# A delta-rule recurrence followed by a gated FFN: the first g @ w_out for four units at once, and the inverses of units 8 and 9 spread over three slots

## The chip, the core and the metric

The kernel runs on one core of a Trainium2 chip. The metric is the device time of one execution in microseconds, from the first to the last instruction and the little that lies around them. The engines are named as in the profile: PE is TensorE's matmul side and PEld its weight loads, DVE is VectorE, ACT is ScalarE, POOL is GpSimd, SP is the engine whose queue issues most DMAs. Each engine works through its own queue in order and waits on semaphores.

## The reference, cut to what matters

Four batches, eight heads, 768 time steps, head dimension 48, then an FFN over 3072 tokens with width 384 and hidden width 2048. The weights come in double precision.

```python
k_n = k / (np.linalg.norm(k, axis=-1, keepdims=True) + 1e-06)
for t in range(S):
    y[:, :, t] = einsum('bhd,bhde->bhe', q[:, :, t], state)
    v_old = einsum('bhde,bhd->bhe', state, k_n[:, :, t])
    state = state + beta_t * einsum('bhd,bhe->bhde', k_n[:, :, t], v[:, :, t] - v_old)
x = y.transpose(0, 2, 1, 3).reshape(B * S, H * D)
h = x @ w_in
g = h * (1.0 / (1.0 + np.exp(-1.702 * h)))
return g @ w_out
```

## The kernel before

**Units.** The recurrence is cut into chunks of 128 steps. A unit is one chunk of one batch, so there are 24 units, in the order chunk first, batch second: units 0 to 3 are chunk 0 of the four batches, 4 to 7 chunk 1, 8 to 11 chunk 2. Inside a unit, a Gram matrix G of the keys is made on PE (`prepare`, `gram`), its four 32 by 32 diagonal blocks per head go through DRAM into a tile NT with one block per partition, DVE inverts them there (`invert`: mostly pairs of a multiply into P and a sum out of P, 25 steps for chunk 2, for two batches at a time), and the inverses come back through DRAM as XB. "Blocks sent" in this document means G's way to NT (`Nd<-G` and `NT<-Nd`).

**A step.** `Step` does one unit: `scores` gives psQ (queries times keys, and keys times state), from which V and the masked matrix M come; then four rounds of `solve` (psU, from XB and V, copied to US by ACT) and `below` (psR, from G and U, subtracted from V by DVE); then `queries` and `outputs` make psY, from which the rows of x (xT) and the new state ST come.

**Slots.** `woven(n)` is one slot of the steady loop. It mixes the last rounds of unit n-1 (A), the middle rounds of unit n (B_) and the scores and first round of unit n+1 (D_), prepares unit n+5 (P, K), takes some steps of an inverse (`ahead_of`, numbers in `STEPS`), and fills the rest of PE's time with FFN work taken from `queue` by `spend`. Slots 3 to 6 take FFN work of cost 13.0 each, later slots 20.8. The order on each engine is the order in which the code records it: the wrapped engines `vec`, `act`, `pe`, `pool` and the wrapped DMA calls `sync` (SP's queue), `beside` (ACT's queue) and `other_queue` (POOL's queue) are pinned to program order.

**The FFN.** `hidden` makes ph = x @ w_in for 256 tokens (two units) and ACT's sigmoid-GELU writes it to gT tiles. `written` makes po = g @ w_out for one unit after another, 16 matmuls each. The queue begins with the rest of `hidden` for units 0 to 3, then `both_written` for units 0 and 1, then `written` for units 2 and 3.

**The weights.** They are turned from double to single precision on the core, piece by piece: `conversions` is a generator of DVE and ACT instructions for w_in's pieces and then for the 16 blocks of w_out, one block being 128 hidden rows by 384. `fill(n)` takes n steps of it; a block is about five steps. `both_written` goes through the blocks feature by feature: for each block it lets the conversion run until the block three ahead is done, and then issues one po matmul for each of two units. `fetch_out` brings a raw block in by DMA; later blocks need the place of earlier ones, and are fetched when those are converted (the table `fetches`), the first eight through POOL's queue and the others through SP's.

**PSUM.** There are eight banks: two in `ps_big` (psT, the first psQ pair, psG), four in `ps_seq` (psU, psR, the second psQ pair, psY), two in `ps_moe` (ph, po).

Of the kernel before, what the change touches and what calls it, by code (L numbers as in the profile page):

```python
# [18 lines left out]
def kernel(  # L19
# [47 lines left out]
    io = ctx.enter_context(tc.tile_pool(name="io", bufs=3))  # L67
    wk = ctx.enter_context(tc.tile_pool(name="wk", bufs=2))
    ps_big = ctx.enter_context(tc.tile_pool(name="ps_big", bufs=2, space=PSUM))
    ps_seq = ctx.enter_context(tc.tile_pool(name="ps_seq", bufs=4, space=PSUM))  # L70
    ps_moe = ctx.enter_context(tc.tile_pool(name="ps_moe", bufs=2, space=PSUM))
    dram = ctx.enter_context(tc.tile_pool(name="dram", bufs=2, space=bass.MemoryType.DRAM))

# [26 lines left out]
    def pinned(op):  # L100

        return lambda *a, **kw: tc.keep_in_program_order(op(*a, **kw))  # L102

    class Engine:

# [75 lines left out]
                )  # L181

    places, slots = {}, {}
    inside = {3: 6, 4: 8, 5: 10, 6: 12, 7: 14, 12: 14, 13: 10}
    outside = {0: "xT", 8: "xT", 11: "xT", 1: "M", 9: "M", 14: "M", 2: "M2", 10: "M2", 15: "M2"}
    order = [0, 1, 2, 3, 4, 5, 6, 7, 8, 13, 9, 10, 12, 11, 14, 15]

    def fetch_out(f):

        if f in outside:  # L190
            slot = outside[f]
            if slot not in slots:
                slots[slot] = wk.tile([128, 2 * DM], I32, tag=slot[:2].strip("2"), name="raw", bufs=3)
            words = slots[slot]
        else:
            words = raws[:, inside[f] * DM : (inside[f] + 2) * DM]
        places[f] = as_raw(words, (1, DM))
        first = order.index(f) < FC // 2
        (other_queue if first else sync)(
            out=as_rows(places[f])[:, 0], in_=moe_w_out[f * 128 : (f + 1) * 128, :]  # L200
        )

# [50 lines left out]
    def conversions():  # L253

        whole = list(pieces())

        def begin(i):
            dst, raw, shape, name = whole[i]
            ops = conversion(dst, places[name[1]] if raw is None else raw, shape)
            next(ops)  # L260
            return ops

        after = begin(0)
        yield
        for i in range(len(whole)):
            ops = after
            next(ops)
            yield
            next(ops)
            yield  # L270
            if i + 1 < len(whole):
                after = begin(i + 1)
                yield
            next(ops)
            yield
            next(ops)
            done.add(whole[i][3])
            fetches.pop(whole[i][3], lambda: None)()
            yield
# [1 line left out]
    fetches = {  # L281
        ("in", 0, 1): lambda: fetch_in(3),
        ("in", 3, 1): lambda: fetch_out(3),
        ("out", 4): lambda: fetch_out(13),
        ("out", 6): lambda: fetch_out(12),
    }
    for new, old in ((8, 0), (9, 1), (10, 2), (11, 8), (14, 9), (15, 10)):
        fetches[("out", old)] = lambda f=new: fetch_out(f)
    converting = conversions()

# [266 lines left out]


    def bank(name, shape=(128, H, D)):
        return ps_seq.tile(list(shape), F32, tag="seq", name=name)  # L560

    lasts = [None]

    class Step:
# [19 lines left out]
        def scores(self):  # L584

            c, S = self.c, slice(128, 128 + D)
            self.QS = (
                spare("QS")[:, 0 : NP * (128 + D)].rearrange("p (j t) -> p j t", j=NP) if self.n == B - 1
                else wk.tile([128, NP, 128 + D], F32, tag="QS", name="QS", bufs=3)
            )  # L590
            transposed(self.qp, self.QS[:, :, 0:128])
            if c > 0:
                St = ST[:, self.b, 0 : NP * D].rearrange("p (j d) -> p j d", j=NP)
                act.activation(self.QS[:, :, S], St, ACT.Copy)
            yield
            self.M = (
                spare("M").rearrange("p (h t) -> p h t", h=H) if self.n in (B - 1, B + 1)
                else wk.tile([128, H, 128], F32, tag="M", name="M", bufs=3)
            )
            n = 128 + D if c > 0 else 128  # L600
            for g in range(0, NP, 2):
                pool_, tag = (ps_seq, "seq") if g else (ps_big, "big")
                ps = [pool_.tile([128, 2, 128 + D], F32, tag=tag, name="psQ") for _ in range(2)]
                for i in range(2):
                    for hh in range(2):
                        r = self.rows(hh)
                        pe.matmul(
                            ps[hh][:, i, 0:n], lhsT=self.kT[r, g + i, :],
                            rhs=self.QS[r, g + i, 0:n], start=True, stop=True,
                        )  # L610
                for hh in range(2):
                    hs = slice(2 * g + hh, 2 * g + 4, 2)
                    if c > 0:
                        Vh = self.V[:, hs, :]
                        vec.tensor_tensor(Vh, Vh, ps[hh][:, :, S], op=ALU.subtract)
                    copy = act.copy if hh == 0 or self.n < 2 * B + HB else vec.tensor_copy
                    copy(self.M[:, hs, :], ps[hh][:, :, 0:128])
                if g == 0:
                    yield
            if self.n >= B:  # L620
                self.select()
# [146 lines left out]
            nc.sync.dma_start(out=out[b * S + c * C : b * S + (c + 1) * C, :], in_=o)  # L768
            yield 1.3

    def both_written(c, gT):

        po = [ps_moe.tile([128, DM], F32, tag="moe", name="po") for _ in range(HB)]
        for n, f in enumerate(order):
            ahead = order[min(n + 3, FC - 1)]
            while ("out", ahead - ahead % 2 if 4 <= ahead < 8 else ahead) not in done:
                fill(1)
            for i in range(HB):
                pe.matmul(
                    po[i], lhsT=gT[f // FQ][:, f % FQ, i * C : (i + 1) * C], rhs=w_out[:, f, :],  # L780
                    start=(n == 0), stop=(n == FC - 1),
                )
            if n < FC - 1:
                yield 1.3
        for i in range(HB):
            o = wk.tile([128, DM], F32, tag="o", name="o")
            act.copy(o, po[i])
            sync(out=out[i * S + c * C : i * S + (c + 1) * C, :], in_=o)
        yield 1.3

    def take(cost):
# [9 lines left out]
    def run(work):  # L801
        for _ in work:
            pass
# [61 lines left out]
            debt[0] -= done  # L865

    STEPS = (9, 5, 3, 3, 3, 3)
    begun = {}

    def woven(n, share):  # L870

        nonlocal inverting
        A, B_, D_ = steps.pop(n - 1, None), steps.get(n), steps.get(n + 1) or NoStep()
        m = n + B + 1
        if n < B + HB:
            K = normalize_mixed(m + 1) if n <= B else iter(())
        else:  # L880
            K = (normalize if n > 6 else normalize_mixed)(m) if m < len(units) else iter(())
        P = prepare(m) if m < len(units) else iter(())
        if m in begun:
            P = begun.pop(m)
        if n % HB == 1 and B < n and n + 1 + HB < len(units):
            inverting = invert(*units[n + 1 + HB], HB)
        ahead = STEPS[:3] if n % HB == 1 else STEPS[3:]

        next(K, None)
        together([(B_, 1)], [(A, 2)])  # L890
        run(D_.scored)
        next(K, None)
        ahead_of(inverting, ahead[0])
        spend(share / 3)

        together([(A, 3), (D_, 0)], [(B_, 1)])
        next(K, None)
        ahead_of(inverting, ahead[1])
        spend(share / 6)
        next(P, None)  # L900
        spend(share / 6)

        together([(B_, 2)], [(D_, 0)])
        if A:
            A.queries()
            A.outputs()
        run(P)
        ahead_of(inverting, ahead[2])
        if n % HB == 0:
            run(inverting)  # L910
        spend(share / 6)
        next(new_step(n + 2).scored, None)
        spend(share / 6)
        follow(n)
# [38 lines left out]
    late_U = room[:, 0 : H * D + XR]  # L953
    pool.memset(late_U[:, H * D :], 0.0)
    zs = room[:, 512 : 512 + 6 * B * H].rearrange("p (s b h) -> p s b h", s=6, b=B)
    psD = [ps_seq.tile([128, B, NP, BS], F32, tag="seq", name="psD") for _ in range(2)]
    warm(NW)
    for b in range(B):
        squares_first(b)
# [133 lines left out]
    load(B + 2, ((QP, q),), sync)  # L1093
    for n in range(2 * B + 1, 2 * B + 1 + HB):
        load(n, ((KN, k),), sync)
    for i in range(22):
        ahead_of(inverting, 1)
        if i < 18:
            feed()
        if i in (2, 3, 4, 7, 8, 9, 10):  # L1100
            fetch_out(i - 2 if i < 5 else i - 3)
    run(inverting)
    def beside_conversion(work):
        for cost in work:
            fill(2)
            yield cost

    queue = [beside_conversion(w) for w in ffn] + [both_written(0, gTs[0]), written(*units[HB], gTs[1])]
    for n in range(B - 1, len(units) + 1):
        woven(n, 20.8 if n > 6 else 13.0)  # L1110
    run(take(1e9))
# [31 lines left out]
```

## Time and profile before

| | us |
|---|---|
| median of 6 runs (772.1 to 779.09) | 773.0 |
| the profiled execution | 772.62 |
| its span, first to last instruction | 770.9 |
| PE busy / DVE busy / ACT busy / POOL busy in the span | 746.5 / 438.8 / 240.0 / 127.8 |
| mean granted PE clock | 0.970 of full |

The page splits the span into 40 slices and gives the busy tenths of each engine; a stretch of any length can be asked for by itself ("windows"). The timeline lists single instructions with start, duration and, in brackets, the idle time before them and what ended it. In the records a po, ph, psQ or psG matmul counts twice and a transpose (psT) once: a po group "x4" is two matmuls of the code.

By the timeline's first small solve of each slot, slot 3 begins at 126.38 us, slot 4 at 138.18, slot 5 at 161.53, slot 6 at 192.04 and slot 7 at 214.03. Before slot 3 lie the loading, the units 0 to 3 and most of the first `hidden`.

### The profile page before, as it was taken

The numbers are of one execution on the slowest core, as the hardware profiler recorded it, in microseconds if no ns is written. First come the engines' busy times: TensorE is split into PE (matmuls) and PEld (weight loads), VectorE is DVE, ScalarE is ACT, GpSimd is POOL, SyncE is SP. The second block draws the span as 40 slices with busy tenths as digits, with TensorE's granted clock in tenths as the row PEclk, the third lists the DMA queues.
The fourth block names the chain that finished last, engine by engine and source line by source line (L and its number), as shares of the span: only waits on it lengthen the run. The fifth ranks groups of instructions, "written<-read, shape, count | busy, mean of one in ns | idle before, by whom it ended". The sixth has DMA issues, their size and how long they took to land.

```text
span 770.9 us, 19471 instructions
## 1 busy us (share of the span) xinstructions
PE 746.5 (97%) x8508; PEld 559.9 (73%) x8508; DVE 438.8 (57%) x896; ACT 240.0 (31%) x535; POOL 127.8 (17%) x133
## 2 busy tenths in 40 slices
PE   7898999979999999999999999999999999999997
PEld 6677888546687687687678678678678677686774
DVE  6998897996776566566566566565566521000000
ACT  3566523433233133133133124123133132121110
POOL 6133301100222122121131221221210000000000
PEclk8599999999999999999999999999999999999999
DMA  9965355542142142142142142042030020000000
GB/s 167 171 120 111 93 135 124 141 107 78 44 97 57 37 94 56 36 96 56 34 96 57 33 98 56 22 108 57 22 78 11 23 43 2 17 11 1 26 1 21
DMA packets 131638, 50.79 MB, mean 66 GB/s; under 512 B 106432, under 2 KB 127040, under 8 KB 131552
## 3 DMA queue, kind: packets, MB, share of 16 engines
q1 hardware_dynamic: 129152, 41.27, 24.5%
q0 software_dynamic: 2400, 8.26, 4.2%
q8 instruction: 67, 1.10, 0.6%
q14 instruction: 19, 0.16, 0.1%
HBM read 32.08 MB, written 16.25 MB: 63 GB/s over the span
## 4 chain that ended last, share of the span: by engine, by line
PE 88%; DVE 7%; ACT 2%; issue 1%; POOL 0%; DVEq 0%; POOLq 0%; ACTq 0%
PE ph L102 32%; PE po L102 30%; PE psY L102 6%; PE psU L102 5%; PE psQ L102 5%; PE psG L102 4%; PE psR L102 3%; PE psT L102 3%; DVE w_out L102 2%; PE ps_warm L102 2%; DVE tmp L102 2%; DVE P L102 1%; DVE V L102 1%; DVE YB L102 1%; ACT QS L102 0%
## 5 line engine op out<-in xcount | busy, mean ns | idle before, releaser
L102 PE MATMUL po<-w_out,gT 128*128 128x384 f32 x768 | 265.5, 497 | 3.7 <-DVE w_out L102 3.7
L102 PE MATMUL ph<-xT,w_in 128*128 128x256 f32 x1152 | 261.2, 383 | 0.3
L102 PEld LDWEIGHTS ph<-xT,w_in 128*128 128x128 f32 x1152 | 214.8, 190 | 32.5 <-issue 1.7
L102 PEld LDWEIGHTS po<-w_out,gT 128*128 128x128 f32 x768 | 143.0, 192 | 97.4 <-issue 5.4
L102 DVE TENSOR_TENSOR V<-V,psR 128x384 f32<-128x384 f32 (+2 forms) x72 | 40.1, 557 | 194.3 <-PE psR L102 193.9
L102 ACT ACTIVATE gT<-ph 128x512 f32<-128x512 f32 x96 | 56.5, 596 | 150.7 <-PE ph L102 150.6
L102 ACT COPY US<-psU 32x384 f32<-32x384 f32 x92 | 43.2, 470 | 141.8 <-PE psR L102 76.9
L102 DVE TENSOR_TENSOR P<-NT,YB 64x8 f32<-64x8 f32 (+26 forms) x178 | 84.4, 474 | 4.7
L102 PEld LDWEIGHTS psU<-V,XB 32*32 32x32 f32 x1536 | 59.3, 106 | 35.6 <-issue 26.5
L102 DVE TENSOR_REDUCE YB<-P 64x4 f32<-64x8 f32 (+27 forms) x178 | 77.2, 434 | 6.2
L102 PE MATMUL psU<-V,XB 32*32 32x48 f32 x1536 | 70.4, 205 | 3.3 <-DVE V L102 3.3
L102 PE MATMUL psR<-US,G 32*32 32x48 f32 x2576 | 63.2, 205 | 0.5 <-ACT US L102 0.5
L624 POOL TENSOR_SCALAR_AFFINE_SELECT M<-M 128x1024 f32<-128x1024 f32 x20 | 25.5, 1273 | 222.8 <-DVE M L102 160.9
L102 PEld LDWEIGHTS psR<-US,G 32*32 32x32 f32 x2576 | 53.9, 105 | 1.3 <-ACT US L102 0.6
L102 PE MATMUL psQ<-QS,kT 48*128 48x176 f32 (+1 forms) x384 | 38.2, 344 | 5.4 <-ACT QS L102 5.4
L102 PEld LDWEIGHTS psQ<-QS,kT 48*128 48x128 f32 x384 | 31.2, 210 | 9.0 <-ACT QS L102 7.2
L102 DVE TENSOR_TENSOR P<-NT 64x256 f32<-64x256 f32 (+7 forms) x44 | 36.3, 824 | 0.3
L102 DVE TENSOR_REDUCE NT<-P 64x64 f32<-64x1024 f32 (+7 forms) x44 | 35.3, 803 | 1.5
L102 PE MATMUL psG<-kT 48*128 48x128 f32 x384 | 33.0, 311 | 1.4 <-ACT G L102 1.2
L102 ACT COPY o<-po 128x384 f32<-128x384 f32 x24 | 11.5, 479 | 72.5 <-issue 41.0
L87 POOL DMA_DIRECT2D KN<-in_k_dram x13 | 12.4, 953 | 118.0 <-PE psY L102 108.8
L102 ACT COPY M<-psQ 128x256 f32<-128x256 f32 x68 | 22.9, 377 | 26.5 <-DVE V L102 17.5
(102 smaller groups left out, 611.1 us busy)
## 6 DMA issues: line engine op xcount, KB each, us to landing
Nd<-G SPq DMA_DIRECT2D x16, 512.0 KB, 3.5
QP<-in_q_dram SPq DMA_DIRECT2D x24, 192.0 KB, 3.8
V<-in_v_dram SPq DMA_DIRECT2D x24, 192.0 KB, 3.1
out_dram<-o SPq DMA_DIRECT2D x24, 192.0 KB, 1.9
KN<-in_k_dram POOLq DMA_DIRECT2D x14, 192.0 KB, 3.7
NT<-Nd SPq DMA_DIRECT2D x20, 128.0 KB, 2.4
Yd<-YS SPq DMA_DIRECT2D x20, 128.0 KB, 2.4
XB<-Yd SPq DMA_DIRECT2D x20, 128.0 KB, 3.0
```

What stands on the lines that cost most here:

```text
L87: dma(out=dst[n % len(dst)][:, :, 0:D], in_=src[b, :, c * C : (c + 1) * C, :].rearrange("h p d -> p h d"),)
L102: return lambda *a, **kw: tc.keep_in_program_order(op(*a, **kw))
L624: (pool if self.n < B else nc.gpsimd).affine_select(out=self.M, in_=self.M, compare_op=ALU.is_gt, fill=0.0, base=0, pattern=[[0, H], [1, 1 ...
```

## The change

1. `both_written` becomes `all_written`: it holds four po tiles, and after each block of w_out it issues four po matmuls (units 0 to 3) where there were two. `written` for units 2 and 3 goes from the queue. The conversion is kept two blocks ahead, and `fill(3)` is taken after each pair of matmuls.
2. The two more po tiles take two of the four `ps_seq` banks. `ps_seq` becomes two pools of two banks. While `all_written` runs (`turns`), the steps have only the first pool for psU, psR, the second psQ pair and psY; otherwise they take the two pools in turn, one bank from each.
3. The four outputs are copied by ACT and sent through ACT's queue. All fetches of w_out go through POOL's queue; the order of the last eight blocks and the places that they use change, and two of them land in gT tiles that the first features leave free.
4. Unit 9's key norm (`ninth`) is made before slot 3 and its transpose, Gram matrix and blocks' way to NT in slot 3; unit 8's Gram matrix is made just ahead of slot 3. The inverse for units 8 and 9 begins in slot 4: `SOON` gives (0, 4, 5) steps in slot 4, (2, 3, 3) in slot 5 and (3, 3, 4) in slot 6, where it was (9, 5, 3) in slot 5, and (3, 3, 3) and the rest in slot 6. The third group of a slot, and five conversion steps, now stand inside `outputs`, ahead of the state's addition.

```diff
-    ps_seq = ctx.enter_context(tc.tile_pool(name="ps_seq", bufs=4, space=PSUM))
+    ps_seq = [ctx.enter_context(tc.tile_pool(name=f"ps_seq{i}", bufs=2, space=PSUM)) for i in range(2)]
...
+    turns = [0, False, False]
+    def seq(shape, name):
+        if not turns[1]:
+            turns[0] ^= 1
+        return ps_seq[0 if turns[1] else turns[0]].tile(list(shape), F32, tag="seq", name=name)
...
-        first = order.index(f) < FC // 2
-        (other_queue if first else sync)(
+        other_queue(
             out=as_rows(places[f])[:, 0], in_=moe_w_out[f * 128 : (f + 1) * 128, :]
         )
...
-    def both_written(c, gT):
-        po = [ps_moe.tile([128, DM], F32, tag="moe", name="po") for _ in range(HB)]
+    def all_written(c, gTs):
+        turns[1] = turns[2] = True
+        po = [
+            (ps_moe if i < HB else ps_seq[1]).tile([128, DM], F32, tag="moe" if i < HB else "seq", name="po")
+            for i in range(B)
+        ]
         for n, f in enumerate(order):
-            ahead = order[min(n + 3, FC - 1)]
+            ahead = order[min(n + 2, FC - 1)]
             while ("out", ahead - ahead % 2 if 4 <= ahead < 8 else ahead) not in done:
                 fill(1)
-            for i in range(HB):
+            for i in range(B):
                 pe.matmul(
-                    po[i], lhsT=gT[f // FQ][:, f % FQ, i * C : (i + 1) * C], rhs=w_out[:, f, :],
-                    start=(n == 0), stop=(n == FC - 1),
+                    po[i], lhsT=gTs[i // HB][f // FQ][:, f % FQ, i % HB * C : (i % HB + 1) * C],
+                    rhs=w_out[:, f, :], start=(n == 0), stop=(n == FC - 1),
                 )
-            if n < FC - 1:
-                yield 1.3
+                if i % HB == HB - 1 and (n < FC - 1 or i < B - 1):
+                    fill(3)
+                    yield 1.3
+            if f == 3:
+                fetch_out(9)
+                fetch_out(13)
+        turns[2] = False
...
+    SOON = {B - 1: (0, 0, 0), B: (0, 4, 5), B + 1: (2, 3, 3), B + 2: (3, 3, 4)}
...
+        if n == B:
+            inverting = invert(*units[2 * B], HB)
+        elif n % HB == 1 and 2 * B < n + HB and n + 1 + HB < len(units):
             inverting = invert(*units[n + 1 + HB], HB)
         ahead = STEPS[:3] if n % HB == 1 else STEPS[3:]
+        ahead = SOON.get(n, ahead)
...
-            A.outputs()
+            A.outputs((lambda: (fill(5), ahead_of(inverting, ahead[2]))) if n <= B + HB else None)
...
-            fill(2)
+            fill(4 if ("in", 3, 1) in done else 2)
...
-    queue = [beside_conversion(w) for w in ffn] + [both_written(0, gTs[0]), written(*units[HB], gTs[1])]
+    queue = [beside_conversion(w) for w in ffn] + [all_written(0, gTs)]
```

More of the change, by code (lines that the diff above doesn't have):

```diff
@@ L183 @@
     places, slots = {}, {}
-    inside = {3: 6, 4: 8, 5: 10, 6: 12, 7: 14, 12: 14, 13: 10}
-    outside = {0: "xT", 8: "xT", 11: "xT", 1: "M", 9: "M", 14: "M", 2: "M2", 10: "M2", 15: "M2"}
-    order = [0, 1, 2, 3, 4, 5, 6, 7, 8, 13, 9, 10, 12, 11, 14, 15]
+    inside = {3: 6, 4: 8, 5: 10, 6: 12, 7: 14, 14: 10, 15: 12}
+    outside = {0: "xT", 8: "xT", 12: "xT", 10: "xT", 1: "M", 2: "M2", 9: "gT", 11: "gT", 13: "gT2"}
+    order = [0, 1, 2, 3, 4, 5, 6, 7, 8, 14, 15, 9, 12, 13, 10, 11]
     def fetch_out(f):
@@ L191, in fetch_out @@
             slot = outside[f]
-            if slot not in slots:
+            if slot not in slots and slot[:2] == "gT":
+                slots[slot] = spare("raw").bitcast(I32)[:, 0 : 2 * DM]
+            elif slot not in slots:
                 slots[slot] = wk.tile([128, 2 * DM], I32, tag=slot[:2].strip("2"), name="raw", bufs=3)
@@ L255, in conversions, with sent @@
         whole = list(pieces())
+        def sent(i):
+            return i >= len(whole) or whole[i][1] is not None or whole[i][3][1] in places
         def begin(i):
@@ L270, in conversions @@
             yield
+            while not sent(i + 1):
+                yield
             if i + 1 < len(whole):
@@ L283 @@
         ("in", 3, 1): lambda: fetch_out(3),
-        ("out", 4): lambda: fetch_out(13),
-        ("out", 6): lambda: fetch_out(12),
+        ("out", 4): lambda: fetch_out(14),
     }
-    for new, old in ((8, 0), (9, 1), (10, 2), (11, 8), (14, 9), (15, 10)):
+    for new, old in ((8, 0), (15, 6), (12, 8), (10, 12), (11, 9)):
         fetches[("out", old)] = lambda f=new: fetch_out(f)
@@ L559, in bank @@
     def bank(name, shape=(128, H, D)):
-        return ps_seq.tile(list(shape), F32, tag="seq", name=name)
+        return seq(shape, name)
     lasts = [None]
@@ L596, in scores @@
             self.M = (
-                spare("M").rearrange("p (h t) -> p h t", h=H) if self.n in (B - 1, B + 1)
+                spare("M").rearrange("p (h t) -> p h t", h=H) if self.n == B - 1
                 else wk.tile([128, H, 128], F32, tag="M", name="M", bufs=3)
@@ L601, in scores @@
             for g in range(0, NP, 2):
-                pool_, tag = (ps_seq, "seq") if g else (ps_big, "big")
-                ps = [pool_.tile([128, 2, 128 + D], F32, tag=tag, name="psQ") for _ in range(2)]
+                shape = [128, 2, 128 + D]
+                ps = [
+                    seq(shape, "psQ") if g else ps_big.tile(shape, F32, tag="big", name="psQ")
+                    for _ in range(2)
+                ]
                 for i in range(2):
@@ L769, in written @@
             yield 1.3
-    def both_written(c, gT):
-        po = [ps_moe.tile([128, DM], F32, tag="moe", name="po") for _ in range(HB)]
+    def all_written(c, gTs):
[3 more added lines that the diff above has]
+            for i in range(B)
+        ]
         for n, f in enumerate(order):
-            ahead = order[min(n + 3, FC - 1)]
+            ahead = order[min(n + 2, FC - 1)]
             while ("out", ahead - ahead % 2 if 4 <= ahead < 8 else ahead) not in done:
                 fill(1)
-            for i in range(HB):
+            for i in range(B):
                 pe.matmul(
-                    po[i], lhsT=gT[f // FQ][:, f % FQ, i * C : (i + 1) * C], rhs=w_out[:, f, :],
-                    start=(n == 0), stop=(n == FC - 1),
-                )
-            if n < FC - 1:
-                yield 1.3
-        for i in range(HB):
-            o = wk.tile([128, DM], F32, tag="o", name="o")
+                    po[i], lhsT=gTs[i // HB][f // FQ][:, f % FQ, i % HB * C : (i % HB + 1) * C],
+                    rhs=w_out[:, f, :], start=(n == 0), stop=(n == FC - 1),
+                )
+                if i % HB == HB - 1 and (n < FC - 1 or i < B - 1):
[5 more added lines that the diff above has]
+        turns[2] = False
+        rest = spare("o")
+        for i in range(B):
+            o = wk.tile([128, DM], F32, tag="o", name="o") if i < HB else rest[:, i % HB * DM : (i % HB + 1) * DM]
             act.copy(o, po[i])
-            sync(out=out[i * S + c * C : i * S + (c + 1) * C, :], in_=o)
+            beside(out=out[i * S + c * C : i * S + (c + 1) * C, :], in_=o)
         yield 1.3
@@ L878, in woven @@
         if n < B + HB:
-            K = normalize_mixed(m + 1) if n <= B else iter(())
+            K = normalize_mixed(m + 1) if n == B else iter(())
         else:
@@ L882, in woven @@
         P = prepare(m) if m < len(units) else iter(())
-        if m in begun:
-            P = begun.pop(m)
-        if n % HB == 1 and B < n and n + 1 + HB < len(units):
+        if n <= B:
+            P = prepare(m + 1) if n < B else iter(())
+        if n == B:
+            inverting = invert(*units[2 * B], HB)
+        elif n % HB == 1 and 2 * B < n + HB and n + 1 + HB < len(units):
             inverting = invert(*units[n + 1 + HB], HB)
         ahead = STEPS[:3] if n % HB == 1 else STEPS[3:]
+        ahead = SOON.get(n, ahead)
         next(K, None)
@@ L897, in woven @@
         next(K, None)
+        turns[1] = turns[2]
         ahead_of(inverting, ahead[1])
@@ L905, in woven @@
             A.queries()
-            A.outputs()
+            A.outputs((lambda: (fill(5), ahead_of(inverting, ahead[2]))) if n <= B + HB else None)
         run(P)
-        ahead_of(inverting, ahead[2])
-        if n % HB == 0:
+        if n > B + HB:
+            ahead_of(inverting, ahead[2])
+        if n % HB == 0 and n > B:
             run(inverting)
@@ L955 @@
     zs = room[:, 512 : 512 + 6 * B * H].rearrange("p (s b h) -> p s b h", s=6, b=B)
-    psD = [ps_seq.tile([128, B, NP, BS], F32, tag="seq", name="psD") for _ in range(2)]
+    psD = [seq((128, B, NP, BS), "psD") for _ in range(2)]
     warm(NW)
@@ L1095 @@
         load(n, ((KN, k),), sync)
+    ninth = normalize_mixed(2 * B + 1)
     for i in range(22):
         ahead_of(inverting, 1)
+        if i in (14, 17, 20):
+            next(ninth)
         if i < 18:
@@ L1102 @@
     run(inverting)
+    next(begun[2 * B])
     def beside_conversion(work):
         for cost in work:
-            fill(2)
+            fill(4 if ("in", 3, 1) in done else 2)
             yield cost
-    queue = [beside_conversion(w) for w in ffn] + [both_written(0, gTs[0]), written(*units[HB], gTs[1])]
+    queue = [beside_conversion(w) for w in ffn] + [all_written(0, gTs)]
     for n in range(B - 1, len(units) + 1):
```

## The prediction, made before the changed kernel was run

> **What bounds the kernel now.** I began with the share of the engines over the 40 slices, and asked for the windows of slots 3 to 7 by themselves (columns: length; busy time and instructions of PE, PEld, DVE, ACT, POOL; granted clock; DMA share; GB/s).
>
> ```profile
> PE   7898999979999999999999999999999999999997
> DVE  6998897996776566566566566565566521000000
> ...
> 126.38:138.18 11.80, 11.76 (x133) 8.59 (x133) 9.86 (x24) 5.08 (x10) 0.47 (x1) 1.00 0.55 156
> 138.18:161.53 23.35, 21.39 (x225) 13.31 (x224) 22.67 (x47) 10.57 (x21) 3.24 (x2) 0.93 0.48 135
> 161.53:192.04 30.51, 25.01 (x305) 15.99 (x304) 22.38 (x57) 9.29 (x22) 2.22 (x2) 0.89 0.33 81
> 192.04:214.03 21.99, 21.62 (x306) 14.37 (x305) 17.38 (x29) 6.93 (x18) 5.52 (x4) 1.00 0.21 47
> ```
>
> PE is full from 200 us to the end, so nothing before that is hidden: a microsecond that PE loses is a microsecond of the whole. Slots 5 and 6 hold the same matmuls (305 and 306 records) and take 30.51 and 21.99 us. In slot 4 DVE is busy 22.67 of 23.35 us. So PE's timeline comes next, for what it waits on there.
>
> ```profile
> 138.18 0.86 PE L102 MATMUL psU<-V,XB 32*32 32x48 f32 x16
> 139.80 1.46 PE L102 MATMUL psQ<-QS,kT 48*128 48x176 f32 x16 [0.76 <-ACT QS L102]
> 141.20 7.12 PE L102 MATMUL po<-w_out,gT 128*128 128x384 f32 x16
> ...
> 159.66 0.66 PE L102 MATMUL psT<-ident,QP 128*128 128x128 f32 x4 [1.08 <-ACT G L102]
> ...
> 164.25 1.77 PE L102 MATMUL psQ<-QS,kT 48*128 48x176 f32 x16 [1.84 <-ACT QS L102]
> 165.95 5.47 PE L102 MATMUL po<-w_out,gT 128*128 128x384 f32 x12
> 175.08 2.54 PE L102 MATMUL po<-w_out,gT 128*128 128x384 f32 x4 [3.66 <-DVE w_out L102]
> ```
>
> The reader is to see two losses. One is waiting: 0.76 + 1.08 + 1.84 + 3.66 = 7.34 us, behind ACT, whose queue holds a conversion step that waits for DVE, or behind DVE itself. The other is the clock: the po group at 141.20 took 7.05 us to the next group; the same sixteen in slot 6 (194.24 to 199.59) took 5.35.
>
> **What can be won.** Against slot 6 without its 0.37 us of waiting (21.62), slot 5 loses 30.51 - 21.62 = 8.9 us. Slot 4 has slot 6's matmuls without the 48 psY records (2.07 us), 19.55, and loses 3.8. Slot 6's own wait adds 0.4. Together 13.1 us: 7.34 + 0.37 of waiting, the rest the clock (three stretches of about 1.7 us, the 7.05 against 5.35 being one). Without any loss the profiled 772.62 would be 759.5.
>
> **Part 1, four po tiles.** The number of po matmuls stays at 384. Each converted block now feeds four of them, 2.64 us of PE (slot 6 pays 0.33 per record), where it fed two, 1.32. A block costs DVE about 2.2 us (from the first step at 159.40 to that of the next at 161.60). So a block of conversion no longer outlasts its matmuls, and the waits "<-DVE w_out" go: the 3.66. In the built order the last block is converted about one slot and a half before its matmul. What covers it is that surplus; gone, the 3.66 would be back.
>
> **Part 2, two banks for the steps.** No row shows a step with two banks, so I bound it. psY takes two banks. In slot 6 psY began at 206.35, when psU and psR of the last round were not yet read; ACT's copy ran 206.39 to 206.86, and DVE's subtraction 206.49 to 207.04. With two banks psY's first bank waits for the copy and its second for the subtraction: at least 0.6 us, if both engines are free. If DVE is in the middle of a pair of the inverse (0.94 + 0.94 us for the 768 wide one), psY waits up to 0.14 + 1.88 + 0.55 = 2.6. DVE does carry conversion or inverse there in slots 5 and 6, so I take the upper half: 2.0 each, 4.0 together (1.2 to 5.2). Behind psY on PE stands all the rest of the slot.
>
> The second psQ pair of slots 4 to 7 needs the banks of the round before it in the same way. In slots 4 and 6 DVE and ACT are near free: 0.5 us for both (0 to 1.5). In slot 5 the 1.84 wait for QS stays, since the same two conversion steps still precede QS on ACT, and the second pair adds ACT's Relu (0.61) and US copy (0.47): 2.9 (1.8 to 3.5).
>
> **Part 3, slot 7.** `turns` is set back in the middle of a slot, so slot 7's psQ still has two banks, and it waits for a V that stands behind the end of the inverse on DVE. That is one sum. From DVE's subtraction in slot 6's second round (where before DVE had waited 1.46 for PE, so it is in time) the new order has: V and the key norm 1.50, then pairs of the inverse 1.30 + 2.49 + 1.84, V 0.55, 1.31 + 0.85 + 0.78 + 1.31, ST and G 0.97, 1.92 + 2.49, YS 1.24, V 0.56: 19.1 us, all by start-to-start times of the same shapes before. PE needs from there 14.8 us (200.41 to 214.03 less the 0.37, and 0.82 for the solve and 0.70 for the first psQ pair). The difference is 4.3, of which 2.0 is slot 6's psY above; 2.3 is left, and 0.4 for ACT's copy behind it: 2.7 (2.0 to 3.6). Before, with four banks, the same V was first needed 8 us of ph later.
>
> **Part 4, the moved fetches, norms and outputs.** The transpose and Gram matrix of unit 9 move from slot 4 to slot 3: PE pays the same 1.5 us. The four output DMAs on ACT's queue come where ACT has idled; each holds ACT as SP was held, some 0.8 us (1.64 for two), at the end of slot 6; that falls into part 3's wait. Fetches on POOL's queue now stand behind `select` (1.5 us, which waits for ACT's M copies) and the power (1.76): two blocks come late, by the landing of 3.1 us that a single fetch by POOL had. DVE then idles 1.5 to 3 us twice. Before, it waited for no fetch there. This idling is what makes DVE late in slot 5, so it is in the 2.9 and the 2.0 there. The KN wait in slot 6 (0.4) stays.
>
> **The clock.** Before, each of the three places where PE had about 3 us without large matmuls was followed by half clock: small solves 0.86, wait 0.76 and psQ 1.40 make 3.0 us; 0.9 + 1.84 + 1.4 make 4.1; and the 3.66. The new waits fall into such places: in slot 5 0.8 + 2.9 + 1.4 = 5.1, in slot 7 0.8 + 2.7 + 1.4 = 4.9, sure; psY in slots 5 and 6 at 2.0 + 0.9 before psY itself, and slot 4's psQ, perhaps, half of them. That is 3.5 stretches of 1.7: 6.0 (two 3.4, five 8.5).
>
> Here the Trainium skill speaks both ways. "TensorE: Matmul & The Clock Gate", Part 1, says that the clock falls after an idle window of about 3.4 us; the row at 139.80 shows it after a wait of 0.76 us, so as worded it doesn't hold here. By it the clock term would be nothing and the time 770.4. The same page, "A second HAM failure mode: psum-queue depth-cycling", says that short idles from cycling through PSUM banks are enough, which is what this change adds.
>
> **The sum.** 4.0 + 0.5 + 2.9 + 2.7 + 0.4 = 10.5 us of waiting and 6.0 of clock make 16.5, where 13.1 were: 3.4 us longer. 772.62 + 3.4 = 776.0; the median of the runs is 0.4 over the profiled one, so 776.4. By the lower bounds: 1.2 + 0 + 1.8 + 2.0 + 0.4 + 3.4 = 8.8, time 768.7; by the upper ones 5.2 + 1.5 + 3.5 + 3.6 + 0.4 + 8.5 = 22.7, time 782.6.
>
> **The rivals.**
> - *The banks cost little.* DVE, with half the conversion rate asked of it, is always there in time. Left are 0.6 + 0.6 at psY, 1.84 at psQ, 0.4, and one clock stretch: 5.1 us, time 765.0. For it: DVE idles in slots 5 and 6 even before. Against it: part 3's 19.1 us stand in the order whatever happens earlier. Chance 0.20.
> - *The clock stays up.* No wait is as long as 3.66, and no stretch follows: 10.5 us, time 770.4. Against it, the 0.76 row. Chance 0.12.
> - *POOL's queue starves DVE.* Late fetches land in 6.1 us, as the four in a row at 94 us did, in place of 3.1. Two blocks, 3 us each, with DVE the late engine: 6 us more, 782.4. It decides from the point where the landing exceeds about 4 us. For it: POOL's fetch waits behind `select`. Against it: the DMA share in slots 4 and 5 is 0.48 and 0.33, low. Chance 0.13.
> - That the change doesn't do what it says, and PE still waits for w_out, would need DVE to lose a slot and a half: left out.
>
> **How the numbers follow.** The forecast has 0.55, at 776.4 with a range of its own from 769 to 782. A measurement tells about 0.5% from no change, 3.9 us: 769.1 to 776.9. The forecast lies near that upper edge, so I give 0.30 of it to slower and 0.25 to no change. Faster: 0.20, the first rival. Within: 0.25 + 0.12 = 0.37. Slower: 0.30 + 0.13 = 0.43. The range runs from 767, which leaves out most of the first rival, to 782.5, which leaves out half of the third.
>
> **What would show it.** PE's timeline should have no wait "<-DVE w_out" of over a microsecond, and instead waits of psY and psQ on DVE's V or ACT's US in slots 5, 6 and 7, with the granted clock below 1 up to slot 7. DVE should show two idle stretches released by DMA or POOL. Slots 3 to 6, counted to slot 7's ph, should be some 3 us longer. A full clock from 140 us on, or psY with no wait, would make the forecast wrong.

## The result, and the profile after

The changed kernel took 776.55 us (median of 33 runs, 773.0 to 781.93) against 773.24 us for the kernel before (75 runs): a ratio of 1.0048, 95% interval 1.0035 to 1.0061. When both were measured again (12 runs of the changed kernel, 34 of the kernel before), it was 1.001, 0.9989 to 1.0032. The two ratios stand for 3.7 and 0.8 us more, so the change costs some 1 to 4 us; the forecast of 3.4 us more lies at the upper end of that.

The page of the changed kernel, the shares over the 40 slices:

```profile
PE   7889999979989999999999999999999999999998
DVE  6997898876865566566566666666665521000000
...
PEclk7587999989999999999999999999999999999999
```

The dip of PE in the ninth slice (155 to 174 us) is a 7 as before. The twelfth slice (213 to 232 us), where slot 7 begins, is now an 8 where it was a 9; behind it PE is full but for the last slice. The clock row (PEclk, the granted clock in tenths) shows something that the prediction did not speak of: an 8 and a 7 in slices 3 and 4 (39 to 77 us), far ahead of the change, where the page before has nines. That comes back below.

The windows of slots 4 to 6 of the changed kernel (same columns as before):

```profile
142.17:162.13 19.96, 18.26 (x205) 11.56 (x205) 16.96 (x39) 6.13 (x15) 6.78 (x7) 1.00 0.65 165
162.13:190.20 28.07, 25.22 (x304) 16.23 (x304) 18.68 (x49) 9.56 (x22) 3.98 (x4) 0.88 0.22 63
190.20:214.32 24.12, 22.30 (x305) 14.68 (x305) 19.94 (x36) 6.90 (x18) 4.77 (x4) 1.00 0.18 37
```

Slot 4 fell from 23.35 to 19.96 us (1.5 of that is unit 9's matmuls, moved to slot 3), slot 5 from 30.51 to 28.07, and slot 6 rose from 21.99 to 24.12. DVE is no longer full in slot 4. What PE waits on from slot 4 to the start of slot 7, from its timeline:

```profile
155.58 0.20 PE L102 MATMUL psU<-V,XB 32*32 32x48 f32 x1 [0.60 <-DVE V L102]
...
162.13 0.20 PE L102 MATMUL psU<-V,XB 32*32 32x48 f32 x1 [1.10 <-DVE V L102]
...
164.70 1.24 PE L102 MATMUL psQ<-QS,kT 48*128 48x176 f32 x8 [1.70 <-ACT QS L102]
166.51 1.54 PE L102 MATMUL psQ<-QS,kT 48*128 48x176 f32 x8 [0.57 <-ACT US L102]
...
182.02 1.18 PE L102 MATMUL psY<-QS,ST 48*64 48x128 f32 x16 [0.49 <-ACT US L102]
...
205.17 0.43 PE L102 MATMUL psY<-QS,ST 48*64 48x128 f32 x2 [0.49 <-ACT US L102]
206.66 0.66 PE L102 MATMUL psY<-QS,ST 48*64 48x128 f32 x14 [1.06 <-DVE V L102]
...
217.94 1.09 PE L102 MATMUL psQ<-QS,kT 48*128 48x176 f32 x8 [1.96 <-DVE V L102]
```

The 3.66 us behind w_out are gone. In their place stand waits for ACT's US copy and DVE's V, at psQ and psY, where the prediction put them, and two at psU, where it had put none. With 0.27 for KN they sum to 8.24 us, where 7.71 stood before. And DVE's own timeline has two stretches in which it waits for a fetch; POOL's shows the two fetches, each issued as soon as the power (rn) or `select` ahead of it ends:

```profile
154.02 0.36 DVE L102 TENSOR_SCALAR w_out<-w_out 128x384 int32<-128x384 int32 x1 [2.39 <-DMA w_out<-in_moe_w_out_dram]
174.19 0.36 DVE L102 TENSOR_SCALAR w_out<-raw 128x384 int32<-128x384 int32 x1 [2.81 <-DMA raw<-in_moe_w_out_dram]
...
147.73 2.36 POOL L102 TENSOR_TENSOR rn<-ssq,half 128x8 f32<-128x8 f32 x1
150.06 0.60 POOL L102 DMA_DIRECT2D w_out<-in_moe_w_out_dram  x1
...
169.10 1.88 POOL L640 TENSOR_SCALAR_AFFINE_SELECT M<-M 128x1024 f32<-128x1024 f32 x1 [4.52 <-ACT M L102]
170.93 0.56 POOL L102 DMA_DIRECT2D raw<-in_moe_w_out_dram  x1
```

### The profile page after: what moved, and what is told of

Same layout as the page of the kernel before. It is cut to its first block, busy times and chain, and to the rows that moved or that the text cites. A ratio compares the mean times of both kernels' runs of the same rounds, so it can differ in the third digit from the quotient of the medians.

```text
span 774.5 us, 19460 instructions
## 1 busy us (share of the span) xinstructions
PE 752.4 (97%) x8508; PEld 565.3 (73%) x8508; DVE 438.3 (57%) x896; ACT 240.4 (31%) x535; POOL 131.9 (17%) x141
## 4 chain that ended last, share of the span: by engine, by line
PE 79%; DVE 7%; SPq 5%; issue 5%; DMA 2%; POOL 1%; ACT 1%; DVEq 0%; POOLq 0%; ACTq 0%
PE po L102 30%; PE ph L102 27%; PE psY L102 5%; PE psU L102 5%; SPq L102 5%; PE psQ L102 4%; PE psG L102 3%; PE psR L102 2%; PE psT L102 2%; DVE P L102 1%; DVE w_out L102 1%; DVE YB L102 1%; DVE tmp L102 1%; PE ps_warm L102 1%; DMA w_out<-in_moe_w_in_dram 1%
## 5 line engine op out<-in xcount | busy, mean ns | idle before, releaser
L102 PE MATMUL psQ<-QS,kT 48*128 48x176 f32 (+1 forms) x384 | 40.1, 350 | 7.0 <-ACT QS L102 4.4
L102 PE MATMUL psG<-kT 48*128 48x128 f32 x384 | 34.7, 323 | 1.2 <-ACT G L102 1.2
L102 PEld LDWEIGHTS psG<-kT 48*128 48x128 f32 x384 | 29.5, 220 | 3.7 <-ACT G L102 2.1
```

## A measure for the stage

Single profiles of these kernels differ by 3 us for a reason outside the change, so the runs are compared over a stage: from the first matmul of the long ph stretch ahead of slot 3 to the end of slot 8's first psQ, on PE's timeline. From each stage its waits are taken (the bracketed idle times) and 1.7 us for each half-clock stretch in it (a stretch of 3.4 us in which the granted clock is 0.5; one of 6.8 us counts as two); what is left is the work and any wait that carries no bracket. Each row is one profiled execution. Those of sp_fetch, old_steps, outs_sp, into_idle and into_idle_sp were the fastest of their runs, that of sooner_only the slowest.

| kernel | stage begins | stage | waits | half-clock stretches | left |
|---|---|---|---|---|---|
| before | 96.40 | 149.50 | 7.71 | 3 | 136.7 |
| again_before | 99.38 | 149.69 | 9.43 | 2 | 136.9 |
| changed | 98.86 | 151.47 | 8.24 | 3 | 138.1 |
| again_after | 96.28 | 153.02 | 9.61 | 3 | 138.3 |
| two_banks | 96.19 | 152.36 | 8.34 | 3 | 138.9 |
| sp_fetch | 96.49 | 146.07 | 6.26 | 1 | 138.1 |
| sooner_only | 99.23 | 152.79 | 10.24 | 4 | 135.8 |
| old_steps | 99.13 | 152.44 | 9.78 | 3 | 137.6 |
| old_steps_again | 98.77 | 155.75 | 9.65 | 5 | 137.6 |
| outs_sp | 96.17 | 150.35 | 7.01 | 3 | 138.2 |
| steps_moved | 96.21 | 152.19 | 7.66 | 4 | 137.7 |
| into_idle | 95.61 | 147.24 | 5.45 | 2 | 138.4 |
| into_idle_sp | 96.29 | 141.70 | 3.30 | 0 | 138.4 |

The last column falls into two groups: 135.8 to 136.9 for the three profiles of kernels whose steps have four banks (before, again_before, sooner_only), 137.6 to 138.9 for the ten of kernels with two. Within a group, waits and clock stretches account for what separates the kernels. Between the groups they don't, although the stage holds the same 1510 PE records in all 13.

The difference is at psQ and psY. Counted from one record's start to the next, without the bracketed idle times and with half clock counted half, psQ's 80 records in the stage take 7.0 us with four banks and 8.1 to 8.8 with two, psY's 144 take 6.2 and 6.6 to 7.2. In slot 6 the same psQ group, without a bracket in either kernel, reads in the kernel before and in two_banks (below):

```profile
192.84 1.46 PE L102 MATMUL psQ<-QS,kT 48*128 48x176 f32 x16
```

```profile
194.24 1.89 PE L102 MATMUL psQ<-QS,kT 48*128 48x176 f32 x16
```

In slot 7 of into_idle (below) the group takes 2.50 us. There its second pair starts bank by bank, each about 0.05 us after ACT's copy of psU or DVE's subtraction of psR has ended (the timeline of each engine, in short windows):

```profile
211.16 0.47 ACT L102 COPY US<-psU 32x384 f32<-32x384 f32 x1
...
211.68 0.56 PE L102 MATMUL psQ<-QS,kT 48*128 48x176 f32 x2
...
211.76 0.56 DVE L102 TENSOR_TENSOR V<-V,psR 32x384 f32<-32x384 f32 x1
...
212.38 0.86 PE L102 MATMUL psQ<-QS,kT 48*128 48x176 f32 x6
```

So two banks cost more than the brackets say: a pause that is short, or covered by the recorded end of the matmul before it, isn't marked in the timeline.

## The experiments

**The same kernels again.** Two copies without an edit.

> The changed kernel once more, unaltered, for a second profile. Theory (bank waits and the clock that follows them, in slots 4 to 7): the waits of PE from slot 4 to slot 7's psQ are the same nine within 0.2 us each, 8.2 us together, wherever the half-clock stretches fall. Rival (what was lost lies ahead of slot 3, where the first profile was 2.6 us behind, at half clock from about 52 to 69 us): slot 3 begins some 2.6 us late again, near 130 us, with the same long half-clock stretch.

> The kernel before once more, unaltered. If the half clock ahead of slot 3 is a matter of chance in each execution, slot 3 does not begin at 126.4 us again exactly, or the half-clock stretches ahead of it lie elsewhere; if it belongs to the kernel, both are as in the first profile. The waits in slots 4 to 6 should again be 7.3 us together.

again_after: 775.21 us (773.0 to 778.55); again_before: 773.72 us (771.18 to 776.0). The waits of the changed kernel came back within 0.1 us, except that psQ's 0.57 was 0.95 and psY in slot 5 waited a further 0.99; together 9.61, not 8.2. The kernel before waited 9.06 in place of 7.3 (9.43 and 7.71 with the 0.37 for KN), with 1.15 for w_out in slot 4 and 0.62 at psG as new ones. So the sum of the waits moves by over 1 us from one execution of a kernel to the next.

The rival was right about the first two profiles alone: of the 3.6 us between their spans (774.5 and 770.9), 2.5 lie ahead of the stage. But it does not belong to the kernel. The stage began at 96.3 us in again_after and at 99.4 in again_before, the other way round. The windows of again_before and of the kernel before, over the same stretch (the granted clock stands third from the end):

```profile
52.90:69.90 17.00, 17.00 (x192) 13.58 (x184) 13.74 (x22) 11.51 (x30) 7.79 (x5) 0.51 0.51 114
```

```profile
52.90:69.90 17.00, 14.10 (x283) 11.98 (x275) 15.84 (x28) 12.62 (x34) 8.76 (x6) 1.00 0.56 119
```

The same code ran 17 us at half clock in one execution and at full clock in the other. In all 13 profiles the stage begins at 95.6 to 96.5 us without that stretch (8 of them) and at 98.8 to 99.4 with it (5). It shows in the runs, too: of the 34 of the kernel before, the 14 with a mean granted clock of 0.966 or 0.967 have a median of 776.4 us, the 20 with 0.970 to 0.977 one of 772.4; the two profiles of that kernel, with and without the stretch, have 0.966 and 0.970.

**Two banks alone.** The kernel before with only the restriction of banks.

```diff
         together([(A, 3), (D_, 0)], [(B_, 1)])
         next(K, None)
+        turns[1] = B <= n < 2 * B - 1
...
         together([(B_, 2)], [(D_, 0)])
+        if n == B - 1:
+            turns[1] = True
```

(with the two pools and `seq` as in the change)

> The kernel before, with its two po tiles and its order of the inverse and the fetches, but psU, psR, the second psQ pair and psY have two banks alone from the end of slot 3 to the middle of slot 7. It computes the whole result. Bank theory: new waits at the second psQ pair of slots 4 and 5 (2 us and 1 us, for ACT's US copy behind conversion steps) and at psY in slots 5 and 6 (0.5 to 0.7 each); the 3.66 behind w_out shrinks by about what was lost earlier. Time 3 to 6 us over before. Rival (two banks are free, the loss comes from POOL's queue and the order of the inverse): within 1 us of before, and no psY wait.

775.61 us, ratio 1.0029 (1.0007 to 1.0051); the stage is 2.7 to 2.9 us longer than in the two profiles before. New waits on PE:

```profile
142.76 0.86 PE L102 MATMUL psQ<-QS,kT 48*128 48x176 f32 x6 [2.01 <-ACT US L102]
...
167.36 1.17 PE L102 MATMUL psQ<-QS,kT 48*128 48x176 f32 x4 [1.08 <-ACT US L102]
...
185.59 0.65 PE L102 MATMUL psY<-QS,ST 48*64 48x128 f32 x10 [0.49 <-ACT US L102]
...
208.67 0.84 PE L102 MATMUL psY<-QS,ST 48*64 48x128 f32 x16 [0.49 <-ACT US L102]
```

They sum to 4.07, at the four places and of the sizes expected, and the wait behind w_out fell to 1.39. The rival is out by the waits at psY; the time alone, 0.5 to 3.9 us over, wouldn't show it. The time rose by 2.2 us (0.0029 of 773.7), below the 3 to 6 us expected. All bracketed waits together are 8.34 us, between the 7.71 and 9.43 of the kernel before, with as many or one more half-clock stretch: most of the longer stage is in the unmarked part, where psQ takes 8.7 us for 7.0.

**The fetches back on SP's queue.**

```diff
-        other_queue(
+        first = order.index(f) < FC // 2
+        (other_queue if first else sync)(
             out=as_rows(places[f])[:, 0], in_=moe_w_out[f * 128 : (f + 1) * 128, :]
```

> The changed kernel with the last eight fetches of w_out on SP's queue again, all else as changed. Theory (DVE is late in slot 5 since two fetches stand behind select and the power on POOL's queue): DVE's idle stretches of 2.4 and 2.8 us before w_out steps go, PE's waits at slot 5's start (1.10 and 1.70) shrink by half or more, and the time falls by 2 to 4 us, to 773 or 774. Rival (those idle stretches are covered): the DVE idle goes, the time stays at 776 to 777.

771.54 us, ratio 0.9963 (0.9942 to 0.9984) to the kernel before. In its profile, which is of the fastest of the 11 runs (769.14), DVE no longer waits for any fetch of w_out, the waits of 0.60 and 1.10 for V are gone, psQ's 1.70 is 1.05, and one half-clock stretch is left of three:

```profile
159.86 0.87 PE L102 MATMUL psQ<-QS,kT 48*128 48x176 f32 x8 [1.05 <-ACT QS L102]
161.68 0.87 PE L102 MATMUL psQ<-QS,kT 48*128 48x176 f32 x8 [0.95 <-ACT US L102]
```

Against the 775.21 of the changed kernel, measured at the same time, that is 3.7 us: one line of the change costs some 4 us, and without that line the change is a gain of 1.2 to 4.5 us over the kernel before. How much of the 4 us is wait and how much clock in a run of middling time, no profile shows.

**The sooner inverse alone.** Part 4 on top of the kernel before, with two po tiles.

```diff
+        if n == B:
+            inverting = invert(*units[2 * B], HB)
...
+        ahead = SOON.get(n, ahead)
```

(with `ninth`, the moved `prepare` and the third group of steps inside `outputs`)

> The kernel before with the fourth part of the change alone: unit 9's norm, transpose and Gram matrix a slot sooner and the inverse of units 8 and 9 from slot 4 on, with two po tiles, four banks and the old fetches. Theory: DVE, which was busy 22.67 of 23.35 us in slot 4, now has the inverse's first eleven steps ahead of conversions that are due at once, so PE waits for w_out in slot 4 already and longer at slot 5's psQ (about 10 to 11 us together where 7.3 were): 2 to 5 us slower than before, 775 to 778. Rival (the sooner inverse is what helps, and all_written costs): faster than before by 2 us or more.

774.47 us, ratio 1.0026 (1.0005 to 1.0047), which is 2.0 us slower. In the profile, the slowest of its ten runs (778.32), PE waited 0.88 and 3.27 us for w_out in slot 4 and 4.32 at slot 5's psQ. The theory has the places, and its sizes are a little too large: 8.5 us of waiting there for 10 to 11, and a time just under the 775 to 778. The rival is out: without the slower use of the blocks, the sooner inverse gains nothing.

```profile
160.13 5.46 PE L102 MATMUL po<-w_out,gT 128*128 128x384 f32 x8 [3.27 <-DVE w_out L102]
...
172.44 1.84 PE L102 MATMUL psQ<-QS,kT 48*128 48x176 f32 x10 [4.32 <-ACT QS L102]
```

**The old inverse under four po tiles.** The changed kernel with the inverse's steps where they were.

```diff
-        if n == B:
-            inverting = invert(*units[2 * B], HB)
-        elif n % HB == 1 and 2 * B < n + HB and n + 1 + HB < len(units):
+        if n % HB == 1 and B < n and n + 1 + HB < len(units):
...
-        ahead = SOON.get(n, ahead)
...
```

(with the third group of steps behind `outputs` again)

> The changed kernel with the inverse of units 8 and 9 as before: from slot 5, steps 9, 5, 3, then 3, 3, 3 and the rest, at their old places. Theory (DVE is the engine that comes late at psY and psQ with two banks): the waits move and their sum stays, nine steps stand in front of slot 5's last V, so psY there waits 3 to 5 us in place of 0.5, while slot 4's and 5's earlier waits shrink; the time is within 1.5 us of the changed kernel. Rival (spreading the inverse is what makes the change bearable): 4 us or more over it.

> old_steps once more, since its four undisturbed runs (777.45 to 781.88) lay over what its profile showed (waits and stage as long as the changed kernel's). If its waits set the time, 776 to 778; if the old place of the inverse costs what those four runs say, 779 or more, and the profile shows a wait or a half-clock stretch that the first one did not.

779.85 us (1.0099, 1.0066 to 1.0131) and, again, 779.73 us (1.0085, 1.0062 to 1.0108). The theory had the waits right and the time wrong. The waits sum to 9.78 and 9.65, as in again_after, but one of them, at psY in slot 5 as expected, is long (4.38 in the first profile, and in the second):

```profile
183.75 1.13 PE L102 MATMUL psY<-QS,ST 48*64 48x128 f32 x14 [4.22 <-DVE V L102]
```

In the second profile a half-clock stretch of three times 3.4 us begins within that wait, at 182.7 us; five in the stage make 8.5 us. The first profile, the fastest of its runs (777.45), had three. So spreading the inverse is worth some 4 us (3 to 7 by the ratios). That these are mostly clock and not waiting is what the second profile suggests: two stretches more than in the changed kernel, 3.4 us, at the same sum of waits.

**Slot 7: DVE's work, ACT's outputs.** Three kernels on the changed one. The first sends the outputs through SP's queue; the second moves four steps of the inverse into the 4.6 us that DVE idles at the end of slot 5; the third, into_idle, does both.

The outputs (outs_sp, into_idle):

```diff
-            beside(out=out[i * S + c * C : i * S + (c + 1) * C, :], in_=o)
+            sync(out=out[i * S + c * C : i * S + (c + 1) * C, :], in_=o)
```

The steps (steps_moved, into_idle):

```diff
-    SOON = {B - 1: (0, 0, 0), B: (0, 4, 5), B + 1: (2, 3, 3), B + 2: (3, 3, 4)}
+    SOON = {B - 1: (0, 0, 0), B: (0, 4, 5), B + 1: (2, 3, 3), B + 2: (3, 3, 0)}
...
+        if n == B + 1:
+            ahead_of(inverting, 4)
```

> The changed kernel with its four outputs sent through SP's queue in place of ACT's, nothing else. In the changed kernel ACT reached slot 7's US copy at 217.65 us, behind four copies of po and four DMA issues, and DVE reached V at 217.33: both are late by the same. Theory: ACT alone being earlier changes nothing at psQ, the wait for V stays at 1.9 to 2.0 us and the time within 1 us of the changed kernel's (775 to 777). Rival (ACT's outputs were what held slot 7): the wait falls to under 1 us and the time by 2 us.

> The changed kernel with four steps of the inverse moved into DVE's idle time at the end of slot 5 and none in slot 6's third group, the outputs still on ACT's queue: the other half of into_idle. Theory: slot 6's second psY wait (1.06) goes, but slot 7's psQ now waits about 2 us for ACT's US copy, where it waited for V, and the half-clock stretch there may stay; about 1 us under the changed kernel, and 2 us or more over into_idle's 769.8. Rival (DVE was the only late engine in slot 7): as fast as into_idle.

> The changed kernel with four steps of the inverse moved into the 4.6 us that DVE idles at the end of slot 5 (behind its copy of G), the third group of slot 6 empty, and the four outputs sent through SP's queue in place of ACT's. Theory (slot 7's psQ wait of 1.96 and slot 6's second psY wait of 1.06 are DVE's 19 us of work against PE's 15): both go, 0.5 to 1.2 us is left at slot 7's psQ for ACT's copies of po, and the half-clock stretch in slot 7 goes: 3 to 5 us under the changed kernel. Rival (these waits are covered by something else that is late): within 1 us of it.

outs_sp took 774.08 us (1.001, 0.9987 to 1.0033), the interval of the changed kernel's second measurement. So no time is shown to be won, though its psQ waited only 0.16, as the rival had it. Part of that is the bracket: the psQ group of slot 7 takes 2.51 us with the 0.16 in it (3.91 with the 1.96 in the changed kernel, 1.46 before), so PE lost 1.05 us there in place of 2.45. DVE shows the rest:

```profile
196.64 0.56 DVE L102 TENSOR_TENSOR V<-V,psR 64x384 f32<-64x384 f32 x1 [2.12 <-PE psR L102]
...
215.42 0.56 DVE L102 TENSOR_TENSOR V<-V,psR 32x384 f32<-32x384 f32 x1
```

From one V to the end of the other DVE needs 19.3 us; the changed kernel's pair is 198.91 to 217.89, 19.0. In outs_sp a half-clock stretch fell into slot 6, behind the 1.06 at psY, and PE came 1.7 us later to a V that was no sooner. Here wait and half clock took each other's place under the same DVE sum, so a shrunken wait alone proves nothing.

steps_moved took 774.17 us (1.0006, 0.9984 to 1.0029): the 1.06 went, and psQ waited 0.77 for V and then 0.83 for ACT's US copy, which stood behind four output copies and their DMA issues until 214.19. into_idle took 769.75 us (0.9965, 0.9943 to 0.9988), without a bracket at slot 7's psQ; its 2.50 us for 1.46 show that 1.0 us is still lost there, as the theory had it (0.5 to 1.2). By the ratios each half alone is worth between nothing and some 3 us, both together 3.5 to 6.4: DVE's V (217.33) and ACT's copy (217.65) were late by nearly the same amount.

**Both cures.**

> into_idle and the fetches on SP's queue together. If the two theories hold, their gains add: 6 to 8 us under the changed kernel, 769 or 770, some 3 to 4 us under the kernel before. If either gain was one of the same wait, less than 5 under the changed kernel.

766.89 us (764.31 to 767.24), ratio 0.9915 (0.9893 to 0.9938): faster than both kernels, and 8.3 us under the 775.21 of the changed one, somewhat more than the 6 to 8 expected. The two gains, 3.7 and 5.5 us against the same 775.21, add up to 9.1, so they nearly add. The profile is of the fastest of the six runs (764.31); its stage has five waits, 3.30 us, and no half-clock stretch at all:

```profile
155.00:232.00 77.00, 73.49 (x963) 53.48 (x962) 59.42 (x136) 27.22 (x63) 15.32 (x11) 1.00 0.34 82
```

Its granted clock is 1.00 throughout. The mean granted clock of the whole run is 0.981 there and 0.970 to 0.977 in the five others, so these had half clock somewhere that no profile shows. Three of the five waits are the ones of bank pairs for ACT's US copy (0.95, 0.49, 0.49).

## Why the prediction came out as it did

**The figure was met, the effect is smaller than stated.** 776.4 was forecast and 776.55 measured, but over both comparisons the change costs about 1 to 4 us where 3.4 were stated. The two pairs of profiles put the stage 2.0 and 3.3 us longer, and the stretch after it 0.9 us shorter in both. That the number came so close is in part luck. Of the 3.6 us between the first two spans, 2.5 are the chance half clock far ahead of the stage. In the stage itself waits and clock together, put at 3.4 us over the kernel before, grew by 0.5 in the first pair and 1.9 in the second; the rest of the 2.0 and 3.3, 1.4 us each, are the unmarked pauses, which the sum did not have as such. The mechanism, banks that make psQ and psY wait for DVE and ACT, is what the runs show.

**What could be won** (13.1 us): 7.71 of waits and three stretches of 1.7 make 12.8, and 9.43 with two make 12.8 again. Right, and wait and clock changed places between the two executions. The 0.3 too much is in slot 4: it lacks not only slot 6's psY but 32 small psU and psR records as well (225 against 306 in all), so what it loses is its 1.84 of waits and one stretch, 3.5 us in place of 3.8.

**Part 1.** Right: no wait of PE for w_out is left, and in slot 4 DVE has time.

**Part 2.** The places were right, the sizes too large by the brackets. psY in slots 5 and 6 was put at 2.0 each; measured were 0.49 (1.48 in again_after) and 1.55. Slot 5's psQ was put at 2.9; measured were 2.27 and 2.64. Not foreseen were the waits of 0.60 and 1.10 for V in slots 4 and 5, which come from the first late fetch: without it, in sp_fetch, both are gone. All waits were put at 10.5; 8.24 and 9.61 came with a bracket, and with the 1.4 us of unmarked pauses 9.6 and 11.0.

**Part 3.** 19.1 us of DVE work were summed; 19.0 came. The wait was put at 2.7, and 1.96 came; the whole psQ group, 3.91 us for 1.46, was held up by 2.45.

**Part 4.** This was the term read too lightly. The two idle stretches of DVE were foreseen at 1.5 to 3 us each (2.39 and 2.81 came) but given no price of their own; sp_fetch shows that the queue of these fetches costs some 4 us, as much as the whole change lost or more. The sum had them inside its waits; between the two profiles more than half of the difference is clock (two stretches, 3.4 us, beside 2.0 us of waits), but that of sp_fetch is of its fastest run. The outputs on ACT's queue were said to fall into part 3's wait. They do, but only because both are late; behind an earlier V they hold psQ by themselves, 0.83 us in steps_moved.

**The clock.** 3.5 stretches were put down and 3 came, twice, with slot 5 and slot 7, the two places called sure, among them. In the first profile of the changed kernel the stretches follow waits of 1.70 and 1.96 us, in the second also one of 0.99, and in the kernel before one of 0.76. A wait of this size doesn't bring one each time: the same 0.76 in again_before, at 142.78 us, has none behind it. When it does and when it doesn't stays open.

The Trainium skill's page "TensorE: Matmul & The Clock Gate", Part 1, says that the clock falls after an idle window of about 3.4 us; if only the waits are taken for idle time, the 0.99 to 1.96 us of the changed kernel don't agree. The page's section "A second HAM failure mode: psum-queue depth-cycling" says that short idles from cycling through PSUM banks are enough to make the clock swing; the stretch at 143.7 us in two_banks, behind 0.76 and 2.01 us, agrees, but in the profile of into_idle_sp waits of 0.95, 0.49 and 0.49 for bank pairs leave it at 1.00.

**What was left out.** What is left of the stage grew by 1.4 us, of which the shorter end gives 0.9 back. It isn't work: two_banks has it too (2.0 to 2.2 us), with the same matmuls as before, and sooner_only, with four banks, doesn't. It stands at psQ and psY, as shown above, and is a part of the price of two banks.

**The rivals.** Banks that cost little: out, by two_banks. A clock that stays up: out, with three stretches in both profiles. POOL's queue: its mechanism was at work, inside the forecast and not on top of it; the eight fetches of the changed kernel between 130 and 180 us landed in 3.2 to 5.1 us (median 3.8), not in the 6.1 that this rival took.

## What to carry to other kernels

When a tile takes banks from a pool that others rotate through, list who now waits for whose eviction, and add up what stands in front of that eviction on its engine; here that sum held to 0.1 us (19.1 and 19.0), while the wait worked out from it was 0.3 to 0.7 too long. Compare the length of the waiting group as well as its bracket. Where two engines are late by the same amount, curing one shows little, so try both before dropping an idea. And compare profiles over a stage that begins after any chance event, or a 3 us difference will be put down to the wrong cause.

## What was not expected of the hardware

The same instructions ahead of the change ran either 17 us or not at all at half clock, in 5 of 13 profiles of kernels that are alike or nearly so there, worth 2.5 to 3 us of the whole. By the granted clocks above it goes with a good part of the spread of runs. Half-clock stretches in the stage numbered 0 to 5; without them and the marked waits the stage comes out between 136 and 137 us with four banks and between 138 and 139 with two.
